# One PSUM tile of eight banks for products and score steps, in a two-layer attention and feed-forward kernel

## The chip, the cores and the metric

The kernel runs on one core of a Trainium2 chip. The metric is the device time of one execution in microseconds (us), the median of three runs. Engines are named as the profile names them: PE is TensorE (PEld its weight loads), DVE VectorE, ACT ScalarE, POOL GpSimd, SP the engine that issues nearly all DMAs here.

## The reference

The input is 2048 rows of 512 numbers. Two layers use the same weights. Each layer is a memory-augmented attention in four segments of 512 rows, then a gated feed-forward network (FFN) of width 1792, each behind a layer norm and a residual sum:

```python
for s in range(N):                                  # N = 4 segments of L = 512 rows, H = 32 heads of Dh = 16
    qs, ks, vs = (q[:, :, s].copy(), k[:, :, s].copy(), v[:, :, s].copy())
    logits = jnp.einsum('bhqd,bhkd->bhqk', qs, ks) * scale + mask      # causal within the segment
    p = _softmax(logits, axis=-1)
    a_dot = jnp.einsum('bhqk,bhkd->bhqd', p, vs)
    pq = phi(qs)                                    # phi(t) = t + 1 where t > 0, else exp(t)
    num = jnp.einsum('bhld,bhde->bhle', pq, M)
    den = jnp.einsum('bhld,bhd->bhl', pq, z)[..., None] + 1e-06
    o = g * (num / den) + (1.0 - g) * a_dot
    ...
    M = M + jnp.einsum('bhld,bhle->bhde', phi(ks), vs); z = z + sum of phi(ks)
...
x = x + _A_ref(_layernorm(x), wq, wk, wv, wo, beta)
x = x + gelu(layernorm(x) @ w_gate) * (layernorm(x) @ w_up) @ w_down
# the same two lines a second time
```

Layer norm takes no scale or shift. Everything is bf16 in and out.

## The kernel before

The work is cut into eight stages k = 0 to 7: four segments of the first layer, then four of the second. Each has an attention (class `Att`) and an FFN (class `Ffn`).

**The planner.** The kernel is a Python program that plans the order of its own instructions. `Clocks` and `Engine` keep a clock for each engine with a fixed cost for each instruction (0.2158 us for a product of 512 columns, 1.024 us for an exponential of a score half with 0.09 us of overlap). The loop from line 1527 moves PE's clock on: at each turn it issues either a step of scores, the next instruction of the product that is open, or opens a new product from `items`, a list sorted by due times (`DUE`, `DUE_STEP`, `BIAS`). DVE, ACT, POOL and SP have queues of jobs; an engine takes the job with the least `ready + slack`. What comes out is a fixed order on each engine; on the chip each engine works in that order, and semaphores hold an instruction until its data is there.

**Products** (`product`, line 575) are groups of four matmuls on column tiles of 32. A product of a dense item has four such groups, or fourteen for the down projection. The items are q, k and v projections, `wo`, gate, up, down, the memory products and the flushes (attention weights times v, line 1158). Each writes one PSUM bank, which DVE or ACT then empties (`evict` posts the copy to both; the first that comes to it takes it).

**Steps of scores** (`Att.scores`, line 1052, matmul at line 1079) use row tiles. A step makes scores for four heads in four PSUM banks, as two halves of two banks each. ACT takes the exponential of each half (line 1120, 128 x 1024) into `pt`; POOL masks the diagonal blocks (line 1107); a flush then multiplies with v. There are 147 steps and 294 exponentials.

**PSUM.** Eight banks: four tiles `m0` to `m3` of one bank for items (`M_BANKS = 4`), and two tiles `st0`, `st1` of two banks each for scores. `score_now` issues a step when both `st` tiles are free, or a half step when one is and nothing else is to be done (or in the first stage). The list `banks` holds when each product bank comes free, `st_free` the same for the two score tiles. Where neither a step nor an item is ready and a bank is free, the planner puts in a product of constants (`warm`, line 1559), whose result nobody reads.

**Around it.** The inputs are loaded by SP: segment 0, wk, wq, segment 1 and wv at once; segments 2 and 3 (`X2`, `X3`), wo, gate, up and down weights at planned times. Normalised rows `xn` are turned by DMA (line 540) into `xnT`; for the FFN of stage 0 by PE. `vpair`, a copy of part of `vaug` with rows interleaved, comes by DMA too (line 824).

Of the kernel before, what the change touches and what calls it, by code (L numbers as in the profile page):

```python
# [48 lines left out]
QK_DUE = 0.671  # L49
E_Q = -0.066  # L50
E_K = 0.868

FLUSH_WAIT = -3.429
PIECE_SLACK = 3.531
URGENT, SOON, NORMAL = -12.202, 0.717, 0.0
EXP_SLACK, E_SLACK, PHI_SLACK, GELU_SLACK = -3.207, 5.725, 8.246, 5.125
ACT_EVICT, FIRST_EVICT = 2.39, -0.102
# [4 lines left out]
RAWS = [7, 8, 8, 7, 11, 11, 9]  # L62
FLUSH_FIRST = -7.633
SECOND_EVICT = -0.274
E_BUFS = 2
KB_SLACK = 10.544
HALF_STEPS = 1
LAST_FIRST = 8
RUSH = 0
# [3 lines left out]
MIX_SLACK, MIX = 0.0, 0.63  # L73
MEM_SLACK = -2.508


DUE = {"wo": 0.367, "gate": 1.082, "up": 1.296, "down": 1.774, "upd": 0.003, "mem": 0.257, "v": 0.079}
DUE_STEP = {"gate": 0.0259, "up": 0.0235, "down": 0.114}
BIAS = {
    **{("qk", *k): d for k, d in {  # L80
# [4 lines left out]
    }.items()},  # L85
    **{("mem", *k): d for k, d in {
        (0,): 0.334, (0, 0): -0.413, (1,): -0.094, (1, 0): 0.014, (2,): 0.141, (2, 0): -0.298, (3,): 0.144,
        (3, 0): -0.001, (4,): -0.233, (4, 0): -0.246, (5,): -0.245, (5, 0): -0.055, (6,): -0.101, (6, 0):
        0.015, (7,): -0.291, (7, 0): 0.048
    }.items()},  # L90
    **{("down", *k): d for k, d in {
# [4 lines left out]
    }.items()},  # L96
    **{("upd", *k): d for k, d in {
        (0,): -0.628, (0, 0): 0.188, (1,): 1.267, (1, 0): 1.014, (2,): -0.343, (2, 0): 0.003, (3,): 0.937,
        (3, 0): -0.543, (4,): -0.419, (4, 0): 0.055, (5,): 0.506, (5, 0): -0.155, (6,): 0.023, (6, 0):
        0.288, (7,): 0.107  # L100
    }.items()},
    **{("v", *k): d for k, d in {
# [4 lines left out]
    }.items()},  # L107
    **{("wo", *k): d for k, d in {
# [4 lines left out]
    }.items()},  # L113
    **{("gate", *k): d for k, d in {
# [6 lines left out]
    }.items()},  # L121
    **{("up", *k): d for k, d in {
# [5 lines left out]
    }.items()},  # L128
    **{("num", *k): d for k, d in {
# [254 lines left out]
def kernel(  # L384
# [70 lines left out]
    def bank_tile(i, shape, dtype=F32):  # L455
        return psp.tile(shape, dtype, tag=f"m{i}", bufs=1, name="m")
# [1030 lines left out]
    def score_now(idle=False):  # L1487
        if not streams:
            return ()
# [6 lines left out]
        if all(free):  # L1496
            return (0, 1)
# [97 lines left out]
```

## Time and profile before

| what | value |
|---|---|
| runs, us | 544.49, 544.31, 544.62 (median 544.49) |
| span of the profiled execution, first to last instruction, us | 543.6 |
| the profiled execution's own device time | not given apart; the median lies 0.9 us over its span |
| PE busy, us (share of the span) | 534.9 (98%) |
| DVE, ACT, POOL busy, us | 427.5, 423.4, 239.5 |
| granted TensorE clock | 1.00 in every stretch |
| DMA | 31.03 MB, mean 57 GB/s |

Busy times are sums over an engine's instructions. Matmuls are pipelined, so PE's busy time counts what overlaps once, and a busy PE may still be doing work that is not wanted (the products of constants) or that costs more than it has to.

### The profile page before, as it was taken

Reading aid. Unit: us, or ns where it says so; the run is one execution under the profiler, and the core shown is the slowest. Engines: PE = TensorE matmul, PEld = TensorE weight load, DVE = VectorE, ACT = ScalarE, POOL = GpSimd, SP = SyncE. Lnnn points to the kernel's source line nnn. Section 1 sums busy time; section 2 is a strip of 40 time slices with the busy share of each in tenths; the row PEclk is TensorE's granted clock in tenths of the full one; section 3 lists DMA queues with packets and bytes.
Section 4 is the critical chain, followed back from the end, with each engine's and each line's share of the span. In section 5 each row is a group of like instructions: output and inputs, shape, how many; then the busy total and the mean of one; then the engine's idle time right before and its main releaser. Section 6 shows DMA issues by size and latency. Waiting matters only on the chain.

```text
span 543.6 us, 28016 instructions
## 1 busy us (share of the span) xinstructions
PE 534.9 (98%) x12664; PEld 272.9 (50%) x12664; DVE 427.5 (79%) x818; ACT 423.4 (78%) x513; POOL 239.5 (44%) x508
## 2 busy tenths in 40 slices
PE   8999989999999999999999999999999999999997
PEld 3444445545444544444444444544544445544994
DVE  7989976989959799888577988689887897675632
ACT  5999989979999779888797577976789866964330
POOL 3776553548535574644432246343573353322000
PEclk9999999999999999999999999999999999999999
DMA  7357611631651124502130222123331014101101
GB/s 232 60 132 192 179 35 33 129 72 24 79 63 22 34 41 71 83 3 45 21 53 12 41 56 28 24 42 62 64 68 23 2 22 81 22 2 51 34 5 41
DMA packets 73575, 31.03 MB, mean 57 GB/s; under 512 B 59440, under 2 KB 73008, under 8 KB 73456
## 3 DMA queue, kind: packets, MB, share of 16 engines
q1 hardware_dynamic: 73312, 29.23, 27.8%
q8 instruction: 99, 1.62, 1.3%
q14 instruction: 20, 0.16, 0.1%
q10 hardware_dynamic: 144, 0.01, 0.0%
HBM read 9.71 MB, written 2.10 MB: 22 GB/s over the span
## 4 chain that ended last, share of the span: by engine, by line
PE 93%; DVE 3%; DMA 2%; issue 1%; ACT 1%; POOL 0%; SPq 0%; ACTq 0%
PE m L575 76%; PE st L1079 9%; PE m L1158 6%; DMA vpair<-vaug 1%; DMA phik<-e 1%; ACT pt L1120 1%; PE m L980 1%; DVE vpair L499 0%; DVE e L883 0%; DVE gel L566 0%; PE m L674 0%; DVE st L1399 0%; DVE e L891 0%; DVE x_sb L1257 0%; DVE rdm L915 0%
## 5 line engine op out<-in xcount | busy, mean ns | idle before, releaser
L1120 ACT ACTIVATE pt<-st 128x1024 bf16<-128x1024 f32 x294 | 285.1, 1028 | 65.3 <-PE st L1079 59.1
L1107 POOL TENSOR_SCALAR_AFFINE_SELECT pt<-pt 128x128 bf16<-128x128 bf16 (+3 forms) x390 | 169.5, 452 | 218.5 <-ACT pt L1120 216.6
L575 PE MATMUL m<-xnT,wg_sb 128*32 128x512 bf16 (+1 forms) x2016 | 107.4, 356 | 0.2 <-issue 0.2
L575 PE MATMUL m<-wd_sb,gel 128*32 128x512 bf16 (+2 forms) x1848 | 106.3, 373 | 0.0
L575 PE MATMUL m<-xnT,wu_sb 128*32 128x512 bf16 (+1 forms) x2016 | 104.6, 356 | 0.2 <-DVE gel L1346 0.2
L1346 DVE TENSOR_TENSOR gel<-gel,m 128x512 bf16<-128x512 bf16 x112 | 74.3, 681 | 26.9 <-PE m L575 25.3
L575 PEld LDWEIGHTS <-wu_sb 128*32 128x32 bf16 x2016 | 53.2, 97 | 39.0 <-issue 4.3
L575 PEld LDWEIGHTS <-wg_sb 128*32 128x32 bf16 x2016 | 50.4, 97 | 38.5 <-issue 6.4
L1257 DVE TENSOR_TENSOR x_sb<-x_sb,m 128x512 bf16<-128x512 bf16 (+1 forms) x65 | 42.5, 667 | 33.6 <-PE m L575 33.4
L575 PEld LDWEIGHTS <-gel 128*32 128x32 bf16 x1848 | 45.2, 97 | 43.7 <-issue 5.5
L1183 DVE STREAM_TRANSPOSE byq<-m 128x512 f32<-128x512 f32 x64 | 45.1, 705 | 13.5 <-PE m L1158 12.4
L1311 ACT ACTIVATE gel<-m 128x512 bf16<-128x512 f32 x51 | 28.4, 601 | 18.1 <-PE m L575 17.9
L598 DVE BATCH_NORM_STATS2 st<-x_sb 128x6 f32<-128x512 bf16 x60 | 40.8, 679 | 0.4
L1158 PE MATMUL m<-pt,vaug 128*32 128x64 bf16 (+6 forms) x1088 | 40.8, 272 | 0.1
L1202 POOL TENSOR_TENSOR aT<-aT,amT 128x512 bf16<-128x512 bf16 (+1 forms) x28 | 28.5, 1022 | 25.9 <-DMA amT<-am 17.6
L575 PE MATMUL m<-wv_sb,xnT 128*32 128x512 bf16 x512 | 33.2, 380 | 0.4 <-DVE am L935 0.4
L575 PE MATMUL m<-xnT,wq_sb 128*32 128x512 bf16 x496 | 33.4, 380 | 0.0
L575 PE MATMUL m<-xnT,wk_sb 128*32 128x512 bf16 x496 | 33.4, 380 | 0.0
L1158 PEld LDWEIGHTS <-vaug 128*32 128x32 bf16 x1088 | 23.4, 97 | 17.6 <-issue 2.1
L1079 PE MATMUL st<-q,kf 16*128 16x448 bf16 (+7 forms) x544 | 31.7, 272 | 0.5 <-ACT pt L1120 0.5
L634 DVE TENSOR_SCALAR xn<-x_sb,mv,rs 128x512 bf16<-128x512 bf16 x64 | 29.4, 501 | 3.0 <-POOL rs L621 2.5
L1311 ACT ACTIVATE gel<-gel 128x1024 bf16<-128x1024 bf16 (+1 forms) x33 | 31.2, 1002 | 0.0
(109 smaller groups left out, 592.5 us busy)
## 6 DMA issues: line engine op xcount, KB each, us to landing
out_dram<-x_sb SPq DMA_DIRECT2D x15, 128.0 KB, 1.8
vpair<-vaug SPq DMA_DIRECT2D x14, 136.0 KB, 2.9
wg_sb<-in_B_w_gate_dram SPq DMA_DIRECT2D x8, 224.0 KB, 3.4
kB<-kf SPq DMA_DIRECT2D x28, 64.0 KB, 2.8
wu_sb<-in_B_w_up_dram SPq DMA_DIRECT2D x8, 224.0 KB, 4.3
wd_sb<-in_B_w_down_dram SPq DMA_DIRECT2D x7, 256.0 KB, 4.1
x_sb<-in_A_x_dram SPq DMA_DIRECT2D x3, 512.0 KB, 6.7
xnT<-xn SPq DMA_TRANSPOSE x56, 2.5
```

The costliest lines, as they stand in the source:

```text
L575: nc.tensor.matmul(out[r], lhsT=lhsT[:, r], rhs=rhs, start=start, stop=stop, tile_position=(0, 32 * c))
L598: nc.vector.bn_stats(out=self.st6[:, 0, :], in_=x_sb[:, self.tt0 + j, :])
L634: nc.vector.tensor_scalar(out=xn[:], in0=x_sb[:, self.tt0 + j, :], scalar1=self.mv[:, j, 0:1], scalar2=self.rs[:, j, :], op0=ALU.subtract, ...
L1079: nc.tensor.matmul(out, lhsT=keys, rhs=rhs, start=True, stop=True, tile_position=(32 * j, 0))
L1107: nc.gpsimd.affine_select(out=dv, in_=dv, pattern=[[0, n] for n in dv.shape[1:-1]] + [[2 if r else 1, c]], compare_op=ALU.is_ge, fill=0.0, ...
L1120: 1.024, lambda st=st, tile2=tile2: nc.scalar.activation(out=tile2[:], in_=st[:], func=ACT.Exp, scale=SCALE), told), table="exp")
L1158: nc.tensor.matmul(ps()[32 * j:32 * j + 32, q0 + shift:q1 + shift], lhsT=va[:, ki, h * (DH + 1):h * (DH + 1) + 32], rhs=step["pt"][j // 2] ...
L1183: nc.vector.transpose(out=self.byq[:, c], in_=ps()[:])
L1202: nc.gpsimd.tensor_tensor(out=self.aT[:, b, where], in0=self.aT[:, b, where], in1=self.amT[b][:, where], op=ALU.add)
L1257: ck.dve.post(ck.made(), slack, (0.15 + 0.533 * n / D, lambda: nc.vector.tensor_tensor(out=xt, in0=xt, in1=ps()[:, 0:n], op=ALU.add), lamb ...
L1311: return lambda: nc.scalar.activation(out=out(), in_=in_(), func=ACT.Gelu_apprx_tanh)
L1346: ck.dve.post(ck.made(), NORMAL, (0.683, lambda: nc.vector.tensor_tensor(out=hidden(g, h), in0=hidden(g, h), in1=banked(ps), op=ALU.mult), ...
```

## The change

All of PSUM becomes one tile `psum` of eight banks. An item takes any bank that is free, with preference for one whose neighbour in its pair is in use, and among these the highest (`free_bank`). A step of scores takes any two free pairs. It is issued when two pairs are free and either nothing else is to be done or ACT's queue of started and waiting work is at most `LEAD` = 1.526 us and at least four banks are free. A half step is only left for the first stage, when nothing else is to be done and ACT has nothing waiting. The unused `RUSH` branch goes. All planner numbers have new values: loads (`X3` from 27.0 to 7.27, the others by up to 2.8), slacks, `RAWS` (how many gate tiles are copied out before their gelu), due times and biases.

```diff
-M_BANKS = 4
+BANKS = 8
...
-WO, WG, X2, WU, X3, WD = 32.0, 37.0, 14.0, 49.8, 27.0, 94.0
+WO, WG, X2, WU, X3, WD = 29.198, 35.628, 13.723, 51.306, 7.27, 94.638
...
-N3 = 35.967
+N3 = 36.091
...
-EXP_SLACK, E_SLACK, PHI_SLACK, GELU_SLACK = -3.207, 5.725, 8.246, 5.125
-ACT_EVICT, FIRST_EVICT = 2.39, -0.102
+EXP_SLACK, E_SLACK, PHI_SLACK, GELU_SLACK = -8.396, 4.945, 10.049, 2.846
+ACT_EVICT, FIRST_EVICT = 2.026, -1.227
...
-RAWS = [7, 8, 8, 7, 11, 11, 9]
+RAWS = [7, 8, 7, 6, 11, 8, 8]
-FLUSH_FIRST = -7.633
-SECOND_EVICT = -0.274
+FLUSH_FIRST = -8.217
+SECOND_EVICT = -2.713
...
 HALF_STEPS = 1
+LEAD, SPARE = 1.526, 0
 LAST_FIRST = 8
-RUSH = 0
...
+    psum = psp.tile([P, BANKS, L], F32, tag="psum", bufs=1, name="m")
+
     def bank_tile(i, shape, dtype=F32):
-        return psp.tile(shape, dtype, tag=f"m{i}", bufs=1, name="m")
+
+        n = 1
+        for size in shape[1:]:
+            n *= size
+        bank = psum[:, i, :] if dtype == F32 else psum[:, i, :].bitcast(dtype)
+        if len(shape) == 2:
+            return bank[:, 0:n]
...
-            sts = {n: psp.tile([P, 2, L], F32, tag=f"st{n}", bufs=1, name="st") for n in halves}
+            sts = {n: psum[:, 2 * p:2 * p + 2, :] for n, p in pairs.items()}
...
-                    st_free[n] = a
+                    banks[2 * pairs[n]] = banks[2 * pairs[n] + 1] = a + 0.05
...
-        free = [f <= ck.pe - 0.05 for f in st_free]
+        pairs = [p for p in range(BANKS // 2) if max(banks[2 * p:2 * p + 2]) <= ck.pe]
+        waiting = sum(j[2][0][0] for j in ck.act.jobs if not j[4])
         if half:
-            return (1,) if free[1] else ()
-        if all(free):
-            return (0, 1)
-        other = any(not j[4] and j[0] <= st_free[1] for j in ck.act.jobs)
-        return (0,) if free[0] and (idle and k >= HALF_FROM or k < HALF_STEPS and not other) else ()
...
+            return {1: pairs[0]} if pairs else None
+        if len(pairs) >= 2 and (idle or ck.act.free + waiting - ck.pe <= LEAD and sum(b <= ck.pe for b in banks) >= 4 + SPARE):
+            return {0: pairs[0], 1: pairs[1]}
+        return {0: pairs[0]} if pairs and idle and k < HALF_STEPS and waiting == 0 else None
+
+    def free_bank():
+
+        return min((i for i in range(BANKS) if banks[i] <= ck.pe), key=lambda i: (banks[i ^ 1] <= ck.pe, -i))
```

More of the change, by code (lines that the diff above doesn't have):

```diff
@@ L540, in turn_later @@
         ck.sp.post(t, slack, (1.3, lambda: nc.sync.dma_start_transpose(out=out(), in_=in_()), told))
-    banks = [0.0] * M_BANKS
+    banks = [0.0] * BANKS
     class Psum:
@@ L1050, in ring, with scores @@
             return int(self.steps[t][0][0][1] == BOTH)
-        def scores(self, t, halves):
+        def scores(self, t, pairs):
             k, r = self.k, self.ring(t)
             parts, flushes = self.steps[t]
+            halves = tuple(pairs)
             if halves[0] == 0:
@@ L1524, in score @@
             it.done()
-        return 1 - halves[-1]
+        return 0 if 1 in pairs else 1
     while streams or items or opened or ck.busy():
         ck.serve()
+        assert ck.pe < 2000.0, (streams[:1], [(it.kind, it.due) for it in items[:9]], e_jobs[:2], banks)
         next_e()
-        halves = () if rushed() else score_now()
-        if halves:
-            half = score(halves)
+        pairs = score_now()
+        if pairs:
+            half = score(pairs)
             continue
@@ L1543 @@
             late = ck.pe - (FLUSH_FIRST if ("scores", 0) not in ev else FLUSH_WAIT)
-            got = next((it for it in items if it.kind in ("wo", "turn") and it.k < RUSH and it.ready()), None)
-            got = got or next((it for it in items if (it.kind != "flush" or not streams or it.posted < late
-                                               or any(len(steps_made[r]) - RINGS[r] >= len(steps_done[r]) for r in range(2))) and it.ready()), None)
-            if got:
-                opened = open_item(got)
+            full = any(len(steps_made[r]) - RINGS[r] >= len(steps_done[r]) for r in range(2))
+            it = next((it for it in items if (it.kind != "flush" or not streams or it.posted < late or full) and it.ready()), None)
+            if it:
+                opened = open_item(it)
                 continue
-        halves = score_now(True)
-        if halves:
-            half = score(halves)
+        pairs = score_now(True)
+        if pairs:
+            half = score(pairs)
             continue
-        if min(banks) <= ck.pe:
-            if streams:
-                ps = Psum()
-                ps.bank = min((i for i in range(M_BANKS)), key=lambda i: banks[i])
-                product(ps()[:], warm[:], wide)
-                ck.on_pe(Clocks.MM[512])
-                ps.read(ck.pe)
-                continue
+        if min(banks) <= ck.pe and streams:
+            ps = Psum()
+            ps.bank = free_bank()
+            product(ps()[:], warm[:], wide)
+            ck.on_pe(Clocks.MM[512])
+            ps.read(ck.pe)
+            continue
         ck.pe += 0.05
-        assert ck.pe < 2000.0, (streams[:1], [(it.kind, it.due) for it in items[:9]], e_jobs[:2], banks)
 _INS = ['A_x', 'A_wq', 'A_wk', 'A_wv', 'A_wo', 'A_beta', 'B_x', 'B_w_gate', 'B_w_up', 'B_w_down']
```

62 lines of the change are left out of this document (30 added, 32 removed), and 111 rows, old and new, of the table BIAS.

## The prediction

> **What bounds the kernel now.** I read the page first: busy times and the chain of waits.
>
> ```profile
> span 543.6 us, 28016 instructions
> PE 534.9 (98%) x12664; PEld 272.9 (50%) x12664; DVE 427.5 (79%) x818; ACT 423.4 (78%) x513; POOL 239.5 (44%) x508
> PE 93%; DVE 3%; DMA 2%; issue 1%; ACT 1%; POOL 0%; SPq 0%; ACTq 0%
> ```
>
> PE works through 98% of the span and holds 93% of the chain that ends last. No bank can be worth more than what PE spends on waiting, on work nobody reads, or on work done in dearer form. Next came busy time by stretch (columns: length, busy of PE, PEld, DVE, ACT, POOL, granted clock, DMA).
>
> ```profile
> 11.00:31.00 20.00, 20.00 (x373) 8.44 (x376) 18.15 (x40) 19.03 (x25) 13.90 (x29) 1.00 0.40 97
> 31.00:51.00 20.00, 19.93 (x412) 8.44 (x402) 17.52 (x35) 19.68 (x25) 15.10 (x34) 1.00 0.74 162
> 51.00:79.00 28.00, 25.46 (x572) 12.07 (x572) 24.34 (x52) 25.39 (x33) 14.26 (x32) 1.00 0.48 120
> 79.00:124.00 45.00, 44.68 (x1212) 23.09 (x1204) 37.36 (x71) 40.69 (x51) 20.85 (x46) 1.00 0.37 77
> 124.00:184.00 60.00, 60.00 (x1436) 28.74 (x1428) 49.69 (x97) 55.02 (x68) 32.79 (x68) 1.00 0.35 47
> 184.00:245.00 61.00, 60.34 (x1500) 29.67 (x1500) 54.66 (x106) 52.73 (x64) 34.19 (x72) 1.00 0.29 45
> 245.00:306.00 61.00, 60.86 (x1404) 29.72 (x1396) 46.48 (x90) 48.80 (x58) 23.48 (x58) 1.00 0.19 31
> 306.00:367.00 61.00, 61.00 (x1456) 29.99 (x1448) 50.18 (x91) 47.62 (x56) 25.12 (x58) 1.00 0.25 40
> 367.00:427.00 60.00, 59.82 (x1452) 29.76 (x1448) 50.01 (x95) 48.93 (x57) 26.91 (x57) 1.00 0.27 49
> 427.00:499.00 72.00, 72.00 (x1600) 35.62 (x1600) 52.20 (x98) 51.27 (x56) 27.18 (x38) 1.00 0.16 32
> ```
>
> Two regimes stand here. From 79 us on PE is full. From 11 to 79 us ACT is: 19.03 + 19.68 + 25.39 = 64.1 of 68 us, and here lies most of PE's waste. PE's idle time from 11 to 499 us adds to 0.07 + 2.54 + 0.32 + 0.66 + 0.14 + 0.18 = 3.9 us, 2.5 of it between 51 and 79. Work nobody reads is the products of constants:
>
> ```profile
> L575 PE MATMUL m<-warm x76: 376/379/390, 22.8 to 46.3; 128*32 128x512 bf16 x76
> ```
>
> Here 76 matmuls are 19 products, all between 22.8 and 46.3 us. Then I read the chain in order of time (start, length, what) for the price of a product and of a step:
>
> ```profile
> 282.45 10.14 PE m L575 x188
> 309.71 2.27 PE m L575 x40
> 58.75 0.33 PE st L1079 x8
> 75.66 0.32 PE st L1079 x4
> ```
>
> A run of 188 matmuls, 47 products, takes 10.14 us: 0.216 us each. Ten products between two steps take 2.27 us, 0.11 over 10 x 0.216; so a step costs 0.11 beside its own 0.33. And a half step (x4) takes as long as a whole one (x8). So cutting a step in two costs 0.32 + 0.11 = 0.43 us. PE's timeline shows the halves:
>
> ```profile
> 23.10 0.39 PE L1079 MATMUL st<-q,kf 16*128 16x64 bf16 x4
> 26.00 1.26 PE L575 MATMUL m<-warm 128*32 128x512 bf16 x20
> 68.98 0.30 PE L1158 MATMUL m<-pt,vpair 128*32 128x64 bf16 x16 [1.76 <-DMA vpair<-vaug]
> 74.15 0.39 PE L1079 MATMUL st<-q,kf 16*128 16x320 bf16 x4 [0.51 <-ACT pt L1120]
> 77.06 0.39 PE L1079 MATMUL st<-q,kB 32*128 32x64 bf16 x4
> 77.38 0.40 PE L575 MATMUL m<-xnT,wg_sb 128*32 128x512 bf16 x4
> 77.72 0.39 PE L1079 MATMUL st<-q,kB 32*128 32x64 bf16 x4
> ```
>
> ```profile
> L1120 ACT ACTIVATE pt<-st 128x1024 bf16<-128x1024 f32 x294 | 285.1, 1028 | 65.3 <-PE st L1079 59.1
> ```
>
> The 294 exponentials are 147 steps of two halves. I count 158 score runs in the timeline, so eleven steps are cut: eight between 12 and 50 us, two at 74 and 77 (above, the second with the first gate product between its halves), one at 213.
>
> So the waste that better use of banks or a better order can remove is 19 x 0.216 = 4.1 (constants) + 11 x 0.43 = 4.7 (cut steps) + 3.9 (idle) = 12.7 us at the very most, 2.3% of the span.
>
> **The change part by part.**
>
> *The banks.* Who waits for a bank today? The list of waits says:
>
> ```profile
> ACT pt L1120 <- PE st L1079: 59.1, 74, 5.2
> PE st L1079 <- ACT pt L1120: 0.5, 1, 0.5
> ```
>
> ACT waits 59.1 us for scores, but it has spare time wherever that happens (it is busy 78%); PE waits once, 0.5 us, for a score bank. The shared banks let a step go out while another's exponentials run, so ACT waits less; that shortens nothing where PE is full. The Trainium skill, "TensorEngine Tiling (Array Packing)", section "PSUM Bottleneck", says that tiling speeds TensorE up but not the emptying of PSUM, which may become the bottleneck. By that rule the eight banks would bring their gain all along the kernel; the trace disagrees from 79 us on, where PE is idle 1.3 us in 420.
>
> *Cut steps.* The new rule leaves halves only to the first stage and an idle PE. The three at 74, 77 and 213 us go for certain: 1.3 us. The eight earlier ones partly stand among products of constants, where they displace nothing wanted; I take two of the eight: 0.9. Bounds 1.3 to 4.7; I take 2.2, nearer the low end, since the constants' row covers the same time.
>
> *Products of constants.* They fill two holes, up to 27 and up to 46 us, in which no item is ready. What ends the first is the turned rows of segment 1, on SP's queue:
>
> ```profile
> 18.69 5.34 SPq L540 DMA_TRANSPOSE xnT<-xn  x4
> ```
>
> Four issues in a row end at 24.0 and must land; no bank helps there. What can shrink is the stage: ACT's work in it holds
>
> ```profile
> L1120 ACT ACTIVATE pt<-st 128x1024 bf16<-128x1024 f32 x34 | 32.8, 1048 | 2.1 <-PE st L1079 1.9
> L567 ACT ACTIVATE kf<-m 128x512 bf16<-128x512 f32 x6 | 3.9, 655 | 0.0
> L567 ACT ACTIVATE vaug<-m 128x512 bf16<-128x512 f32 x5 | 2.9, 658 | 0.0
> L567 ACT ACTIVATE q<-m 128x512 bf16<-128x512 f32 x3 | 2.0, 670 | 0.0
> ```
>
> 8.8 us of copies between 11 and 51 us. With EXP_SLACK at -8.4 exponentials go ahead of copies, and DVE must take them; it has 40 - 35.7 = 4.3 us spare there, six copies at most, so ACT could be at most 6 x 0.63 = 3.8 us earlier through the stage, and FFN work, which fills PE, with it. Bounds 0 and 4.1; I take 1.2, nearer to zero because DVE is at 89%.
>
> *Idle.* The wait of 1.76 us for vpair and the 0.5 us are of the old order; a new order removes them or makes others. Old waits gone: 3.9 at most; new ones from 0 up to as many again. I take 1.8 gone (the vpair wait) and 1.3 new: net 0.5.
>
> *Loads.* X3 at 7.27 puts segment 3's load ahead of segment 2's on SP, past the four transposes at 18.69 and vpair's two DMAs. Today they are issued here (and a row of DMA traffic from 0 to 60 us in 40 slices of 1.5 us):
>
> ```profile
> 6.14 1.60 SPq L421 DMA_DIRECT2D x_sb<-in_A_x_dram  x1
> 25.57 0.60 SPq L421 DMA_DIRECT2D x_sb<-in_A_x_dram  x1
> GB/s 0 75 276 219 328 359 358 350 134 15 0 0 0 98 87 88 87 153 254 139 5 87 132 52 90 282 158 182 140 197 179 229 247 186 105 255 57 228 210 129
> ```
>
> SP issues segment 2 at 6.14, as nothing ahead of it waits; both would now go out by about 8 us. 512 KB at 350 GB/s are 1.5 us, into slices 10 to 12 that are empty today (15 to 19.5 us). That cover hides it: 0. Without it, the transposes would be 1.5 us late and the first hole as much longer. The other loads move by under 3 us, tens of us ahead of their first use: 0.
>
> *RAWS* falls by six tiles in all: six copies fewer (0.6 us each) on engines with over 100 us spare: 0.
>
> *Sum.* 2.2 + 1.2 + 0.5 = 3.9 us less: the span goes from 543.6 to 539.7. The median of the runs lies 0.9 us over the span, so the forecast is 540.6 us, 0.7% below. Its own range: with the lesser ends (1.3 of halves, no constants, no idle) 543.2; with the larger (4.7, 1.2, 1.8) 536.8.
>
> **The rivals.** A measurement of this kernel can tell about 0.2%, 1.1 us, from no change.
>
> *ACT's pace holds PE (slower).* PE is in order. A product that takes a bank in which scores stood now waits for an exponential, not for a copy, and behind it on PE stand the rest of that item, the next step and the flush, and behind those DVE's copies. The planner lets exponentials follow each other every 1.024 - 0.09 = 0.934 us. The trace shows
>
> ```profile
> 41.27 9.66 ACT L1120 ACTIVATE pt<-st 128x1024 bf16<-128x1024 f32 x10
> ```
>
> 0.966 us each: ACT falls back 0.03 us with each. Where ACT is full, in stages 0 and 1 (74 exponentials), that adds to 2.4 us, and every such wait now reaches products too. It decides once ACT is more than about 0.3 us, a step's length, behind the plan when a bank is reused, that is after ten exponentials in a row. With the halves' sure 1.3 us back: 544.5 + 2.4 - 1.3 = 545.6; if the new order also makes idle time as large as today's, without removing the old, + 3.9: 549.5. For it: ACT at 94% before 79 us and the one wait at 74.15. Against it: copies and exponentials free today's banks on the same engines, and PE waits little.
>
> *Nothing moves.* The policy keeps one step ahead at most (a step puts 2.05 us on ACT, over LEAD), so PE's work from 79 us on is the same and the holes before are set by DMA: 544.5.
>
> *All waste goes:* halves, constants and idle, less a wait or two: 533 to 536.8.
>
> *The clock falls.* The profile grants 1.00 in all stretches, with today's eight banks cycled in two sets and no PE wait over 2 us. If holes grew so that one stretch, say 51 to 79 us, ran at half clock, its 25.5 us of PE work would double: 570. The Trainium skill, "TensorE: Matmul & The Clock Gate", section "A second HAM failure mode: psum-queue depth-cycling", tells of a kernel that lost clock by cycling through PSUM banks with small idle gaps between groups. By that rule more banks in turn speak against the change; this trace shows no such loss.
>
> **How the numbers follow.** Forecast 0.46; all waste goes 0.12; nothing moves 0.10; ACT's pace 0.30; clock 0.02. Faster: 0.46 + 0.12 = 0.58; same 0.10; slower 0.30 + 0.02 = 0.32. The range leaves out the clock, the last third of the slower case and half of the best: 535.5 to 548.5. The forecast's own range is 536.8 to 543.2.
>
> **What would show it.** Right: eight or more fewer score runs than 158 on PE; fewer than 76 constant matmuls; PE idle from 11 to 499 us under 3.4 us; ACT's wait for scores well under 59 us with the time hardly moved by that; gate products of stage 0 starting before the 77.4 us of today. Wrong: waits of PE on exponentials, copies or DMA that add to more than 4 us; constants beyond 76; a granted clock under 1.00; or a time below 536, which would mean that PE's full stretch after 79 us had slack I do not see.

## The result, and the profile after

| kernel | median us | runs |
|---|---|---|
| before | 544.56 | 4 (544.31 to 544.78) |
| changed | 547.88 | 4 (546.54 to 548.16) |

The ratio is 1.0054, 95% interval 1.0040 to 1.0068: the changed kernel is slower by half a per cent. The profiled execution of the changed kernel took 547.72 us with a span of 546.0, so 1.7 us lie around the span, against 543.6 us of span before. The prediction named 540.6 us and faster.

The page of the changed kernel first: span, busy times and the chain.

```profile
span 546.0 us, 28241 instructions
PE 535.1 (98%) x12736; PEld 275.1 (50%) x12736; DVE 433.0 (79%) x817; ACT 421.5 (77%) x512; POOL 241.6 (44%) x508
PE 93%; DVE 3%; issue 1%; ACT 1%; DMA 1%; POOL 0%; ACTq 0%; DVEq 0%
```

It looks like the page of before: PE is still busy 98% and holds 93% of the chain. Shares hide what happened; the stretches and the constants show it. Columns of the first five rows: length, busy of PE, PEld, DVE, ACT, POOL, granted clock, DMA; then the constants and the gate products.

```profile
51.00:79.00 28.00, 25.63 (x676) 12.32 (x672) 24.60 (x50) 25.68 (x33) 19.70 (x40) 1.00 0.57 126
79.00:124.00 45.00, 44.35 (x1056) 22.59 (x1052) 36.44 (x62) 43.90 (x56) 21.01 (x43) 1.00 0.36 76
184.00:245.00 61.00, 59.21 (x1464) 29.09 (x1457) 53.53 (x103) 46.92 (x56) 30.16 (x66) 1.00 0.26 44
245.00:306.00 61.00, 60.10 (x1340) 29.20 (x1339) 50.14 (x100) 41.21 (x53) 21.28 (x51) 1.00 0.22 34
306.00:367.00 61.00, 60.12 (x1458) 29.16 (x1452) 50.23 (x95) 52.64 (x63) 26.49 (x56) 1.00 0.35 48
L613 PE MATMUL m<-warm x148: 379/379/390, 22.4 to 56.2; 128*32 128x512 bf16 x148
L613 PE MATMUL m<-xnT,wg_sb x2016: 269/379/390, 81.8 to 524.6; 128*32 128x512 bf16 x143, 128*32 128x256 bf16 x41
```

Three things changed on PE.

- **Score runs** fall from 158 to 147 in its timeline: no step is cut any more. By the prediction's price that is 11 x 0.43 = 4.7 us gained.
- **Products of constants** rise from 76 matmuls to 148, from 19 products to 37: 18 x 0.216 = 3.9 us lost, all before 57 us. The first gate product of stage 0 starts at 81.8 us, not at 77.4.
- **PE idle time** from 11 to 499 us rises from 3.9 to 6.6 us (the five stretches above hold 2.37 + 0.65 + 1.79 + 0.90 + 0.88 of it): 2.7 us lost.

Sum: -4.7 + 3.9 + 2.7 = +1.9 us; the span grew by 2.4. Busy time shows what the cut steps were really worth. From 11 us on PE is busy for 525.6 us before (534.9 less 9.35 in the first 11 us) and 525.2 after (535.1 less 9.89). That is 0.4 us less in spite of 3.9 us more of constants, so the cut steps were worth about 4.3 us, 0.39 each. So the cut steps and the constants nearly cancel, and the idle time is what is left.

The new idle time lies in stretches that were almost full before, and the list of PE's waits (in total, times, longest) names it. Before:

```profile
PE m L1158 <- DMA vpair<-vaug: 1.8, 1, 1.8
PE m L674 <- DVE xn L634: 0.5, 1, 0.5
PE st L1079 <- ACT pt L1120: 0.5, 1, 0.5
PE m L575 <- DVE am L935: 0.4, 1, 0.4
PE m L575 <- DVE gel L1346: 0.2, 1, 0.2
```

After:

```profile
PE m L1118 <- ACT pt L1159: 1.8, 3, 1.0
PE m L1197 <- DMA vpair<-vaug: 1.2, 1, 1.2
PE m L1018 <- DMA phik<-e: 1.1, 1, 1.1
PE m L613 <- DVE x_sb L1296: 0.9, 1, 0.9
PE m L1197 <- DVE gel L1385: 0.8, 1, 0.8
PE m L613 <- ACT pt L1159: 0.4, 1, 0.4
```

A PE instruction that waits for an exponential (`pt`), for a product of gelu and up (`gel`) or for a residual sum (`x_sb`) does not wait for data: those instructions read a bank, and PE wants the bank. Such waits are 1.8 + 0.9 + 0.8 + 0.4 = 3.9 us, against 0.5 + 0.4 + 0.2 = 1.1 before. With eight banks to choose from, PE waits more for banks than with two fixed sets.

One more row is new, on ACT:

```profile
ACT pt L1159 <- PE m L1118: 45.0, 51, 6.5
ACT L1159 <- PE m L1118: 17.7, 2, 16.0
```

The first row is the wait for scores, 59.1 us before. The second has no tile: it is a table load that waits for the scores of the exponential behind it. Together they are 62.7 us, so ACT waits no less for scores than before. ACT's timeline shows both loads.

```profile
225.62 1.28 ACT L1159 ACT_TABLE_LOAD   x1 [1.72 <-PE m L1118]
226.91 3.77 ACT L1159 ACTIVATE pt<-m 128x1024 bf16<-128x1024 f32 x4
309.00 1.28 ACT L1159 ACT_TABLE_LOAD   x1 [15.99 <-PE m L1118]
310.30 1.94 ACT L1159 ACTIVATE pt<-m 128x1024 bf16<-128x1024 f32 x2
```

ACT sits idle for 16 us, and then, when the scores are there, first loads the table of exponentials for 1.28 us. The load belongs to the exponential and stands behind the exponential's wait. PE meets the late exponentials at once:

```profile
227.99 0.40 PE L1118 MATMUL m<-q,kf 16*128 16x320 bf16 x8 [1.04 <-ACT pt L1159]
312.29 0.39 PE L1118 MATMUL m<-q,kf 16*128 16x320 bf16 x6 [0.60 <-ACT pt L1159]
```

Before had no table load behind a wait for scores.

### The profile page after: what moved, and what is told of

Its sections match the earlier page's. It is cut to its first block, busy times and chain, and to the rows that moved or that the text cites. A ratio compares the mean times of both kernels' runs of the same rounds, so it can differ in the third digit from the quotient of the medians.

```text
span 546.0 us, 28241 instructions
## 1 busy us (share of the span) xinstructions
PE 535.1 (98%) x12736; PEld 275.1 (50%) x12736; DVE 433.0 (79%) x817; ACT 421.5 (77%) x512; POOL 241.6 (44%) x508
## 4 chain that ended last, share of the span: by engine, by line
PE 93%; DVE 3%; issue 1%; ACT 1%; DMA 1%; POOL 0%; ACTq 0%; DVEq 0%
PE m L613 76%; PE m L1118 8%; PE m L1197 6%; PE m L500 1%; ACT pt L1159 1%; DMA vpair<-vaug 1%; DVE kI L808 1%; PE m L1018 0%; DVE x_sb L1296 0%; DVE byq L1222 0%; POOL pt L1146 0%; DVE ab L1230 0%; DVE gel L604 0%; DVE aT L1237 0%; DVE r L1226 0%
## 5 line engine op out<-in xcount | busy, mean ns | idle before, releaser
L1159 ACT ACTIVATE pt<-m 128x1024 bf16<-128x1024 f32 x294 | 280.5, 1031 | 49.1 <-PE m L1118 45.0
L1146 POOL TENSOR_SCALAR_AFFINE_SELECT pt<-pt 128x128 bf16<-128x128 bf16 (+3 forms) x390 | 171.8, 459 | 193.3 <-ACT pt L1159 191.6
L613 PE MATMUL m<-wd_sb,gel 128*32 128x512 bf16 (+2 forms) x1848 | 108.3, 373 | 1.0 <-DVE x_sb L1296 0.9
L613 PE MATMUL m<-xnT,wg_sb 128*32 128x512 bf16 (+1 forms) x2016 | 105.3, 356 | 0.3
L613 PEld LDWEIGHTS <-wu_sb 128*32 128x32 bf16 x2016 | 52.1, 97 | 40.8 <-issue 5.5
L613 PEld LDWEIGHTS <-wg_sb 128*32 128x32 bf16 x2016 | 52.1, 97 | 39.2 <-issue 5.1
L1350 ACT ACTIVATE gel<-m 128x512 bf16<-128x512 f32 x57 | 31.8, 604 | 18.6 <-PE m L613 18.3
L604 DVE CAST gel<-m 128x512 bf16<-128x512 f32 x39 | 26.6, 684 | 8.0 <-PE m L613 6.8
L613 PE MATMUL m<-wo_sb,aT 128*32 128x512 bf16 x512 | 32.0, 380 | 0.1
L672 DVE TENSOR_SCALAR xn<-x_sb,mv,rs 128x512 bf16<-128x512 bf16 x64 | 27.1, 464 | 4.5 <-POOL rs L659 4.0
```

The source lines that it names most:

```text
L613: nc.tensor.matmul(out[r], lhsT=lhsT[:, r], rhs=rhs, start=start, stop=stop, tile_position=(0, 32 * c))
L672: nc.vector.tensor_scalar(out=xn[:], in0=x_sb[:, self.tt0 + j, :], scalar1=self.mv[:, j, 0:1], scalar2=self.rs[:, j, :], op0=ALU.subtract, ...
L1146: nc.gpsimd.affine_select(out=dv, in_=dv, pattern=[[0, n] for n in dv.shape[1:-1]] + [[2 if r else 1, c]], compare_op=ALU.is_ge, fill=0.0, ...
L1159: 1.024, lambda st=st, tile2=tile2: nc.scalar.activation(out=tile2[:], in_=st, func=ACT.Exp, scale=SCALE), told), table="exp")
L1350: return lambda: nc.scalar.activation(out=out(), in_=in_(), func=ACT.Gelu_apprx_tanh)
```

## The experiments

Five theories were tried. Each experiment ran beside the kernel before on its own chip; the times of before given with a ratio are from there.

- **A, no rest.** `free_bank` takes the highest bank whose neighbour is in use. In the kernel before, an item took the bank that had been free longest. On PE's clock in the planner, 154 of the 524 products of the changed kernel take a bank that came free less than 0.3 us earlier; before it was 32 of 506. A reader that comes a little late on the chip then stops PE.
- **B, the order.** The new order itself runs into more waits for data, whichever banks it uses.
- **C, one tile.** A single PSUM tile makes semaphores coarser.
- **D, whole steps in stage 0.** Before 79 us ACT is full, so cut steps there cost nothing and feed ACT early; without them stage 0 gets longer and the difference comes back as constants.
- **E, table loads.** The loads behind a wait cost PE time.

The planner's own clock for PE (a count of its fixed costs, no time of the chip) ends at 538.4 us before and at 535.9 after. The planned order is better by 2.5 us; the chip takes 6 us more than planned for the one and 12 us more for the other. So the question is where the chip falls behind the plan.

### One tile, old order

The kernel before with all PSUM in one tile, each product and each half step in the bank it had:

```diff
+    psum = psp.tile([P, 8, L], F32, tag="psum", bufs=1, name="m")
...
-            sts = {n: psp.tile([P, 2, L], F32, tag=f"st{n}", bufs=1, name="st") for n in halves}
+            sts = {n: psum[:, 4 + 2 * n:6 + 2 * n, :] for n in halves}
```

> The kernel before, with its order, its banks and its numbers unchanged, but all of PSUM allocated as one tile (items in banks 0 to 3, scores in banks 4 to 7). Theory A (a bank taken again with no slack) and theory B (the new order itself waits for data): nothing moves, 544.5 us within 0.5, PE idle from 11 to 499 us 3.9 us as before. Theory C (one tile makes the semaphores coarser, so PE waits for readers of other banks): slower by 2 to 4 us, with the new waits on PE that the changed kernel shows (exponentials, gelu products, residual sums as releasers).

Measured: 545.54 us against 545.35, ratio 1.0008 (0.9994 to 1.0022). C, which asked for 2 to 4 us, falls: one tile costs nothing that the runs can tell. PE is idle for 2.8 us from 11 to 499 us in this profile and 3.9 in the profile of before. Nearly all of the difference is the wait for `vpair` (0.8 and 1.8 us), so one profile scatters by about 1 us.

### The new order, banks that rest longer

The changed kernel, with the same order on every engine; only which free bank is taken comes from a list made so that as few banks as can be are taken less than 0.3 us after they came free (48 of 524 products):

```diff
+    def next_bank():
+        taken_banks.append(1)
+        return BANK_OF[len(taken_banks) - 1]
...
-                self.t = bank_tile(self.bank, self.shape, self.dtype)
+                self.t = bank_tile(self.place, self.shape, self.dtype)
...
+            places = {n: next_bank() for n in pairs}
...
         it.ps.bank = free_bank()
+        it.ps.place = next_bank()
```

> The changed kernel with the same order on every engine; only the physical bank of each item and each score half is another, from a written-out list chosen so that a bank rests longer between its reader's planned end and its next writer. By the planner's own times 154 of the 524 items take a bank that has rested under 0.3 us in the changed kernel, 32 of 506 in the kernel before, and 48 of 524 in this one. Theory A: PE's waits for DVE and ACT reading a bank (3.9 us in the changed kernel: 1.8 scores, 0.8 flush, 0.9 down, 0.4 up) fall to about 1.5 to 2.5 us and the time from 547.9 to 545.5 to 546.5 us. Theory B: the waits move to the next thing that is late, and the time stays at 547.9 within 0.6. Theory C: as B.

Measured: 546.77 us, ratio 1.0030 (1.0019 to 1.0041). The changed kernel, taken again on the same chip, is the measure for it:

> The changed kernel once more, beside the others on the same chip: 547.9 us within 0.8, PE idle from 11 to 499 us 6.6 us within 1, by all theories.

It gave 548.55 us, ratio 1.0054 (1.0041 to 1.0067). The banks alone give back 1.8 us of its 3.2 by the medians, 1.3 of 2.9 by the ratios. The list of PE's waits of the kernel with the list:

```profile
PE m L1137 <- ACT pt L1178: 1.6, 3, 0.8
PE m L1036 <- DMA phik<-e: 1.4, 1, 1.4
PE m L1216 <- POOL pt L1165: 1.1, 1, 1.1
PE m L631 <- ACT pt L1178: 0.4, 1, 0.4
```

The waits for `x_sb` and for `gel` (0.9 and 0.8) are gone from its head. The waits behind the table loads stay, as they must: the order is the same. A wait of a flush for POOL's mask is new, so the idle time of this one profile (6.7 us) is no smaller; what is smaller is the time of six runs.

### The old order, banks that rest less

The reverse: the kernel before, same order, but each product takes the product bank that came free last (145 of 506 under 0.3 us).

> The kernel before with the same order on every engine and its separate tiles; only the bank of each item among its four is another: of those that are free, always the one that came free last, from a written-out list. By the planner's own times 145 of the 506 items then take a bank that has rested under 0.3 us (32 before). Theory A: PE gets waits for copies, gelu products and residual sums of 1 to 3 us in all, and the time goes from 544.5 to 545.5 to 547.5 us. Theory B and theory C: 544.5 within 0.5.

Measured: 547.89 us, ratio 1.0053 (1.0038 to 1.0068), as slow as the changed kernel. In its profiled execution (549.83 us) PE is idle for 6.0 us from 11 to 499 us, not 3.9. The third of these rows stood in the list of before; the others were shorter or absent:

```profile
PE m L590 <- DVE am L950: 0.7, 1, 0.7
PE m L1173 <- DVE gel L581: 0.6, 1, 0.6
PE st L1094 <- ACT pt L1135: 0.5, 1, 0.5
PE m L590 <- DVE gel L1361: 0.5, 1, 0.5
```

They add up to 2.3 us, against 1.1 before; a wait of 0.8 us for `kB`, a DMA, makes up most of the remaining idle time. Here nothing but the choice among free banks differs from the kernel before, and it costs 547.89 - 545.35 = 2.5 us. A is shown in both directions.

### Whole steps and half steps in stage 0

The kernel before, with no half steps in stage 0:

```diff
-HALF_FROM = 0
+HALF_FROM = 1
-HALF_STEPS = 1
+HALF_STEPS = 0
```

> The kernel before, planned by its own numbers, but with no half steps in stage 0 (whole steps alone, as the changed kernel makes them there). Everything behind stage 0 is planned anew without being tuned, so only stage 0 is read. Theory D (halves cost PE nothing in stage 0, because ACT sets its length; without them ACT gets its exponentials late and the time comes back as products of constants): the last exponential of stage 0 ends after 59 us (54.8 before) and the constants rise well over 19 products. By my prediction's price of a cut step (0.43 us each, won back): stage 0 ends at 54 us or earlier with 19 or fewer.

And the changed kernel, with a half step in stage 0 whenever one pair is free:

```diff
-        return {0: pairs[0]} if pairs and idle and k < HALF_STEPS and waiting == 0 else None
+        return {0: pairs[0]} if pairs and k < HALF_STEPS else None
```

> The changed kernel with half steps allowed in stage 0 whenever one pair is free, also while ACT has work waiting. Later stages are planned anew and not tuned, so only stage 0 is read. Theory D: the last exponential of stage 0 ends at 51 to 54 us (58.5 in the changed kernel) and fewer than 37 products of constants are left. By the price of a cut step: stage 0 ends later than 58.5.

Both are replanned all through by that one change, so only stage 0 is read, not the whole time (555.89 and 549.79 us, one run each). Constants and first gate products, without halves:

```profile
L575 PE MATMUL m<-warm x236: 376/379/390, 21.9 to 62.0; 128*32 128x512 bf16 x118
L575 PE MATMUL m<-xnT,wg_sb x2016: 272/379/390, 88.1 to 532.8; 128*32 128x512 bf16 x143, 128*32 128x256 bf16 x41
```

and with them:

```profile
L613 PE MATMUL m<-warm x120: 379/379/390, 25.9 to 73.9; 128*32 128x512 bf16 x120
L613 PE MATMUL m<-xnT,wg_sb x2016: 269/379/390, 74.2 to 526.6; 128*32 128x512 bf16 x143, 128*32 128x256 bf16 x41
```

Taking the halves from the kernel before moves the first gate product from 77.4 to 88.1 us and the constants from 76 to 236 matmuls. Giving them to the changed kernel moves it from 81.8 to 74.2, and the constants from 148 to 120. The last exponential of stage 0 ends at 64.8 us without halves and 55.9 before, at 53.1 with halves and 59.6 in the changed kernel (the 54.8 and 58.5 us that the expectations name are its starts). D is shown for stage 0: while ACT is the engine that is full, a cut step costs PE only time that it has, and half a step is what ACT needs next.

### The rule of the key, and the rule without its numbers

The changed kernel with the bank that has been free longest, replanned:

```diff
-        return min((i for i in range(BANKS) if banks[i] <= ck.pe), key=lambda i: (banks[i ^ 1] <= ck.pe, -i))
+        return min((i for i in range(BANKS) if banks[i] <= ck.pe), key=lambda i: (banks[i ^ 1] <= ck.pe, banks[i]))
```

> The changed kernel with one key changed in free_bank: among banks whose neighbour is in use (or among the others), the one that came free longest ago in place of the highest. The plan changes with it: the planner's own PE clock ends at 541.0 in place of 535.9 (538.4 for the kernel before, which took 544.5 on the chip, 6 us more; the changed kernel took 12 us more). Theory A: with rested banks the chip follows the plan about as well as with the kernel before, 546.5 to 549 us, and PE's idle time from 11 to 499 us is under 5.5 us. Theory B: the distance from plan to chip stays at 12 us, 553 us.

Measured: 549.75 us, ratio 1.0097 (1.0065 to 1.0128). The plan ends at 541.0 here, so the chip is 8.7 us behind it, not 12: the rest shows, but another key gives another plan, and this one is worse by 5.1 us, with 54 products of constants. PE is idle for 5.4 us from 11 to 499 us. The numbers were found for one key and do not serve another. The time lies 0.75 us over what A expected.

The new rule with the planner numbers of before:

> The new rule for banks and steps with the planner's numbers of the kernel before (loads, slacks, due times, biases). The planner's own PE clock ends at 544.1. Theory A: the bank rule brings its waits with any numbers, so the chip takes 10 to 12 us more than the plan: 554 to 556 us, PE idle from 11 to 499 us 6 us or more. Theory B (the waits belong to the new numbers): 550 us, 6 us more than the plan as with the kernel before.

Measured: 554.51 us, ratio 1.0165 (1.0130 to 1.0201); plan 544.1, so 10.4 us behind; 62 products of constants. That is where A put it, not B. The rule, with numbers found for another rule, loses 9 us, and the new numbers win back two thirds of that.

### The table loaded ahead

An activation of one column, on constants, ahead of each switch of tables. It waits for nothing, so the load goes out when ACT comes free:

```diff
+    ck.act.switched = lambda table: nc.scalar.activation(
+        out=tick[:], in_=warm[:, 0:1], func=ACT.Exp if table == "exp" else ACT.Gelu_apprx_tanh)
```

In the changed kernel:

> The changed kernel with the same order, and on ACT one added activation of 128 x 1 (constants in, scratch out, no wait) ahead of each operation that needs another activation table, so that the table is loaded when ACT has finished what stands before, not when the operation's scores have come. In the changed kernel two of the table loads to exp stand behind a wait for scores (17.7 us of idle time, at 225.6 and 309.0 us), and PE's waits of 1.04, 0.18 and 0.60 us for exponentials follow them; in the kernel before no table load stands behind a wait for scores. Theory E (these two loads make the exponentials 1.28 us late each, which the planner does not count): the time falls by 1.5 to 2.5 us from the changed kernel's, to 1.001 to 1.003 of the kernel before, and PE's waits for exponentials fall from 1.8 us to under 0.9. Theory A alone (bank rest is all of it): no change beyond 0.5 us, ratio 1.0054 as before.

Measured: 547.83 us, ratio 1.0055 (1.0033 to 1.0076): no gain, to within about 1 us. The profile does what it should; ACT's timeline at the same place as above:

```profile
291.38 1.28 ACT L723 ACT_TABLE_LOAD   x1
292.67 0.21 ACT L723 ACTIVATE tick<-warm 128x1 bf16<-128x1 bf16 x1
307.28 1.94 ACT L1166 ACTIVATE pt<-m 128x1024 bf16<-128x1024 f32 x2 [14.40 <-PE m L1125]
```

The exponentials follow their scores at once, and PE's wait of 1.8 us on them leaves its list. The gain is real in this profile up to 312 us and partly gone by 345, in a wait for `kB` and small waits for banks. E alone does not move the time by the 1.5 to 2.5 us that were expected.

Together with the list of banks:

> The changed kernel with both: rested banks from the written-out list and the tables loaded ahead. Theories A and E together: the two gains add (1.5 from the banks, about 2 from the tables), 3 to 4 us under the changed kernel: ratio to the kernel before 0.998 to 1.000. If they are the same waits seen twice: no better than the better of the two alone, 1.002 to 1.003.

Measured: 545.64 us against 545.30 for the kernel before, ratio 1.0002 (0.9988 to 1.0016). The same order as the changed kernel, with banks that rest and tables loaded ahead, loses nothing any more against the kernel before. The tables are worth about 1.5 us here (1.0030 to 1.0002, on two chips) and nothing that shows where the banks are tight. That time gained ahead of a tight bank is lost again at the bank would explain this; no run shows it. And the plan is not reached: this kernel takes 9.7 us more than its plan of 535.9, the kernel before 6.9 more than 538.4 on this chip. So A and E account for the loss against the kernel before, but about 2.8 us of the plan's gain stay open, and B is not excluded for them.

The kernel before with tables loaded ahead:

> The kernel before with the same added activations. No load to exp waits for scores there, so theory E expects no gain: the same within 0.5 us (ratio 0.999 to 1.001).

Measured: 545.20 us, ratio 1.0002 (0.9992 to 1.0012). It had no load behind a wait for scores, and gains nothing.

### The load of segment 3

The changed kernel with `X3` back at 27.0, the order on the computing engines the same:

> The changed kernel with segment 3 of the input loaded at X3 = 27.0 as in the kernel before; the order on PE, DVE, ACT and POOL is the same, only SP's differs. My prediction's step (moving the load costs nothing): ratio as the changed kernel, 1.0054, within 0.001. If the early load delays transposes or phi's DMA in stage 0 or 1: faster by 0.5 to 1.5 us, with PE's wait for phik (1.1 us at 65 us) gone.

Measured: 548.50 us, ratio 1.0061 (1.0045 to 1.0077). The moved load costs nothing and gains nothing, to within about 1 us.

### Planned with rest

If the loss is slack that the plan does not leave, the plan should ask for it. The rule of the changed kernel, but the planner takes a product's bank as free 0.25 us after its copy instead of 0.05, and a pair of scores 0.1 us after its exponential; halves in stage 0 whenever a pair is free; the margins for `phik` and `kB` 0.5 us larger; planner numbers searched anew against the planner's clock alone; the list of banks and the tables ahead:

```diff
-            banks[self.bank] = t + 0.05
+            banks[self.bank] = t + (REST if self.rest else 0.05)
...
-        return {0: pairs[0]} if pairs and idle and k < HALF_STEPS and waiting == 0 else None
+        return {0: pairs[0]} if pairs and k < HALF_STEPS else None
```

> The changed kernel with everything the runs so far name, planned anew: an item's bank counts as free 0.2 us later than in the changed kernel and a score pair 0.05 us later, half steps are allowed in stage 0 whenever one pair is free, phi's and vpair's DMAs are given 0.5 us more, the due times and biases are searched anew for that (in the planner alone), the physical banks come from a list that rests them, and tables are loaded ahead. The planner's own PE clock ends at 536.9 (538.4 before, 535.9 changed). Theories A, D and E together: the chip follows the plan as closely as with the kernel before or closer (5 to 7 us more): 542 to 544 us, ratio 0.995 to 0.998. If what was lost in the changed kernel belongs to shared banks as such: ratio 1.003 or more.

Measured: 540.52 us against 545.59, ratio 0.9913 (0.9890 to 0.9936): faster than both kernels, and by more than the theories gave. Page, PE's waits for banks and first gate product:

```profile
PE 531.0 (98%) x12588; PEld 270.4 (50%) x12588; DVE 422.6 (78%) x807; ACT 426.2 (79%) x537; POOL 242.9 (45%) x508
PE m L1737 <- ACT pt L1778: 1.3, 3, 0.5
PE m L1227 <- ACT pt L1778: 0.7, 2, 0.4
L1227 PE MATMUL m<-xnT,wg_sb x2016: 272/379/390, 73.7 to 513.6; 128*32 128x512 bf16 x143, 128*32 128x256 bf16 x41
```

No row of constants is left in its stage 0 (37 x 0.216 = 8.0 us in the changed kernel), and PE is busy 4.1 us less; the rest went back into cut steps, eleven as in the kernel before, all before 50 us. PE's idle time from 11 us to the end falls by 2.5 us, from 9.8 to 7.3. So the larger part of the gain over the changed kernel is stage 0, not rest. Against the kernel before all of it is busy time: from 11 us on PE is busy for 521.1 us instead of 525.6, about the 4.1 us of the 19 products of constants there, and idle for 7.3 us instead of 7.0. Stage 0 is 8 us shorter than in the changed kernel by its first gate product. The plan ends at 536.9, later than the changed kernel's 535.9, and the chip takes 4 us more than planned instead of 12.

Another search of the same kind, with the bank that has been free longest as the key (the expectations call the kernel above o1 and this one o2):

> As o1, another search, with the bank that came free longest ago chosen in the planner as well. PE clock of the plan 536.9. Theories A, D and E: ratio 0.995 to 0.998; shared banks as such: 1.003 or more.

Measured: 542.53 us, ratio 0.9955 (0.9936 to 0.9973). Then this order again without the list of banks and without the activations on constants:

> The plan of o2 with the same order on every engine, without the written-out bank list and without the added activations of 128 x 1. If the rest that the plan gives is enough (35 of 493 items under 0.3 us by the plan's own choice of banks), within 0.1% of o2; if a table load still stands behind a wait for scores, slower than o2 by up to 1 us for each.

Measured: 543.08 us, ratio 0.9952 (0.9934 to 0.9970), the same. With rest in the plan, the list of banks and the activations add nothing that the runs can tell. One table load still stands behind a wait here,

```profile
ACT L1944 <- DVE x_sb L1890: 10.0, 1, 10.0
```

with no cost that the time shows.

### The same plan without the sharing

What of this gain is the sharing, and what the rest and the new search? The kernel before with its two fixed sets, but with the same rest, margins, activations on constants and a search of the same 40 minutes:

```diff
-            banks[self.bank] = t + 0.05
+            banks[self.bank] = t + (REST if self.rest else 0.05)
...
-                    st_free[n] = a
+                    st_free[n] = a - 0.05 + SREST
```

> The kernel before with its two fixed sets of banks, planned as the kernel with rest was: a product's bank counts as free 0.25 us after its copy and a score tile 0.1 us after its exponential, margins for phik and kB 0.5 us larger, planner numbers searched anew for the same 40 minutes against the planner's clock alone, tables loaded ahead. Its plan ends at 541.4 us, where the shared banks came to 536.9 and the kernel before, without rest, to 538.4. If the shared banks are what the gain of the kernel with rest needs, this one stays 3 to 6 us behind it on the chip, as the plans do: 543.5 to 546.5 us, ratio to the kernel before 0.997 to 1.002. If the rest and the search alone gave the gain, it comes to 541 or less, ratio 0.993 or lower.

> The kernel with shared banks planned with rest, taken again beside the searched kernel before on one chip: ratio to the kernel before 0.989 to 0.994 as in its first run. The difference between the two is read from this call alone. If the shared banks carry the gain, 3 to 6 us lie between them; if rest and search do, under 1.5 us.

Measured: 548.73 us, ratio 1.0069 (1.0045 to 1.0094), for the fixed sets; 541.30 us, ratio 0.9940 (0.9922 to 0.9958), for the shared banks: 7.4 us between them. The first is slower than both theories gave it. It has 32 products of constants, and its stage 0 is long:

```profile
PE 537.6 (99%) x12716; PEld 277.4 (51%) x12716; DVE 431.8 (79%) x821; ACT 424.1 (78%) x525; POOL 241.1 (44%) x508
L1170 PE MATMUL m<-warm x128: 376/379/391, 23.0 to 73.4; 128*32 128x512 bf16 x128
L1170 PE MATMUL m<-xnT,wg_sb x2016: 272/379/391, 80.5 to 524.2; 128*32 128x512 bf16 x143, 128*32 128x256 bf16 x41
```

Its span is 545.6 us and PE is idle for 6.9 us of it from 11 us on, no more than the 7.3 of the kernel with shared banks. The two profiles differ in busy time, 537.6 and 531.0 us, and 32 x 0.216 = 6.9 us of constants cover that. So what the shared banks gave these searches is a shorter stage 0. That four product banks cannot do it is not shown: the kernel before, with four and no rest, has 19 products of constants.

Nor did rest bring this kernel nearer to its plan: it takes 7.3 us more than its 541.4, the kernel before 6 to 7 more than its 538.4. So the choice of a rested bank is shown to be worth time in a fixed order, but the value of rest in the plan by itself is not. Two limits stay. One search for each is few, and a longer one may find a better plan for the fixed sets. And against the changed kernel the faster one has rest, margins, halves in stage 0, tables ahead and new numbers at once, which were not tried one by one in it.

## Why the prediction was wrong

The range held the time; the sign was wrong. Forecast were gains of 2.2 us from cut steps, 1.2 from constants and 0.5 from idle time. Measured were about 4.3 gained, 3.9 lost and 2.7 lost: the first two nearly cancel, and the idle time is what made the kernel slower. Step by step:

**Cut steps: their price was nearly right, their consequence was missed.** The sum counted on five, the signs asked for eight, and all eleven went, at about 0.39 us each. The step "I take two of the eight", with bounds that were all gains, failed. It had ACT full before 79 us and cut steps at that place side by side and did not join them: where ACT sets the pace, the half is what feeds ACT. What it left out was the loss: the first gate product comes 4.4 us later, and constants fill the time.

**Products of constants: wrong in sign.** Predicted 1.2 us gained, measured 3.9 lost. The bounds had zero as the worst end. Without halves, stage 0 is longer and has nothing to fill it with: the run without them in the old order has 59 products of constants.

**Idle: wrong in sign.** Predicted 0.5 gained, measured 2.7 lost. The step that failed is "PE waits once, 0.5 us, for a score bank", taken as proof that banks do not bind. It read the score banks alone; the same list has 0.6 us for product banks. They hardly bound because most had rested before they were used again. The diff shows the change of that, `key=lambda i: banks[i]` to a key with `-i`, and the prediction did not price it. The old order with the tight choice shows its size: 2.5 us, with nothing else changed. The table loads behind waits, 1.5 us once the banks rest, are the other part, and no step of the prediction has them.

**Waits of ACT for scores: wrong.** "ACT waits less" did not come true. The row fell from 59.1 to 45.0 us, but 17.7 us for the same scores now stand ahead of table loads, 62.7 in all. With tables loaded ahead and rested banks the row itself is 60.8 us. So no run shows what a shorter wait of ACT would have done to the time.

**Loads: right**, 0 to within about 1 us, by the run with `X3` at 27.0. The one tile, which the prediction gave no price, costs nothing either. The six copies of `RAWS` were not tried by themselves.

**The rival "ACT's pace holds PE"** gave 545.6 to 549.5 us, and the time lies there. Its mechanism is only a part: products that wait for an exponential are 0.4 us of the 3.9. Steps that wait for one are 1.8, mostly behind the table loads that no rival named; products and flushes that wait for DVE are 1.7. Its thought that PE is in order, so that a late reader of a bank now stops everything behind it, was the right one, and the prediction set it aside because PE waited little in the trace of before.

**The clock** stayed at 1.00 in the changed kernel, as the forecast had it.

**What would show it**: gate products of stage 0 before 77.4 us, constants under 76, idle under 3.4 us all came out on the wrong side; the fall in score runs alone came true. The first sign of a wrong prediction, waits of PE on exponentials, copies and DMA over 4 us, came true, and so did constants beyond 76. The 0.9 us around the span, a median against another run's span, is 1.7 us where both are of one execution. So the profiled execution of the kernel before took about 545.3 us, above its median, and the medians lie 3.3 us apart where the spans differ by 2.4.

## What to carry to other kernels

Slack that a trace shows is a property of the order in it: one wait of 0.5 us for a bank says that the banks as they were taken did not bind, and nothing about another way of choosing among the free ones. In a schedule that is fixed ahead, taking the buffer that came free last gains nothing over taking the one that has been free longest, and it makes a late reader a stop of the engine that fills it: that cost 2.5 us here in one order and 1.3 to 1.8 in another. Letting the plan count a buffer as free a little late was tried only together with other changes. And a piece of work that looks dear on the full engine can be cheap in a stage where another engine is full.

## What the runs showed of the hardware

**A table load takes part in the wait of the operation behind it.** 16 us of idle ACT ahead of one are not used for it (rows at 309 us above). An activation of one column ahead of it costs 0.21 us and moves the load into the idle time.

**The granted clock fell without a long pause of PE.** In the profile of the changed order with rested banks and tables ahead, the clock is 0.50 for 3.4 us, from about 240.0 to 243.4. Stretches around it (columns as above), and PE's timeline:

```profile
235.00:239.00 4.00, 2.72 (x71) 1.25 (x63) 3.85 (x9) 0.00 (x0) 3.31 (x3) 1.00 0.65 103
239.00:241.00 2.00, 1.66 (x21) 0.68 (x25) 0.78 (x3) 1.20 (x2) 0.11 (x1) 0.76 0.31 62
241.00:243.00 2.00, 2.00 (x24) 0.85 (x20) 0.98 (x3) 1.25 (x2) 0.73 (x2) 0.50 0.04 7
243.00:246.00 3.00, 3.00 (x56) 1.19 (x52) 2.83 (x7) 1.89 (x3) 0.55 (x2) 0.93 0.01 3
239.34 0.39 PE L1144 MATMUL m<-q,kB 32*128 32x64 bf16 x5 [1.24 <-DMA kB<-kf]
239.66 4.03 PE L634 MATMUL m<-wo_sb,aT 128*32 128x512 bf16 x40
```

The ten products at 239.66 take 4.03 us instead of 10 x 0.216. Before that PE was busy 2.72 us of four, and its longest wait was 1.24 us. The Trainium skill, "TensorE: Matmul & The Clock Gate", section "Why this matters for your kernels", advises against idle gaps of PE of more than about 3 us; no such gap stands here. The Trainium skill, "TensorE: Matmul & The Clock Gate", section "A second HAM failure mode: psum-queue depth-cycling", tells of a clock that falls by small idle gaps between groups of matmuls, which is nearer to this trace. But a wait of 1.76 us in the kernel before (at 68.98 us) left the clock at 1.00, so the wait of 1.24 us is not shown to be what made it fall. In the kernel with rest in its plan alone, five of ten runs had a mean clock of 0.993 or 0.994 and took 543.4 to 544.4 us, and the five with a clock of 1.000 took 541.0 to 542.7; where their clock fell, no profile shows.
